# Turning q by VectorE in blocks of 32 partitions, the left tokens attended along, and buffers given by urgency

## The chip, the cores and the metric

The kernel runs on one core of one Trainium2 chip. The metric is the time of one execution on the device, in microseconds (us). Everything is in float32. A core has TensorE (PE, matrix products), VectorE (DVE), ScalarE (ACT), GpSimd (POOL), SyncE (SP, which issues most transfers) and 16 DMA engines.

## What is computed

Linear attention with a norm, and then a mixture of four experts of two layers each:

```
kv  = einsum('bhsd,bhse->bhde', k, v)            # batch 8, heads 8, seq 576, head_dim 64
out = einsum('bhsd,bhde->bhse', q, kv)
rms = sqrt(mean(out * out, axis=-1) + 1e-06)
att = out / rms * g_norm
x   = att with heads side by side                # 4608 tokens x 512
p   = domain_probs / (domain_probs.sum(-1) + 1e-09)
y   = sum over e of p[:, e] * (relu(x @ w1[e]) @ w2[e])   # w1: 512 x 1024, w2: 1024 x 512
```

Each batch has 576 tokens. The kernel works on blocks of 512, so the first 512 tokens of each batch make one block ("chunk" c = 0 to 7), and the 64 **left tokens** of all eight batches make a ninth. There are 36 stages: four experts times nine chunks. Attention runs only in the stages of expert 0: while stage s does the MoE work of chunk s, the attention of batch s + 1 is done beside it. The x of each chunk is stored to DRAM for the later experts.

## The kernel before

The MoE products use a scheme with fewer products and more additions (sums and differences of blocks, made by VectorE and GpSimd), over two levels in most stages. All its products go through one helper, which gives TensorE the two column halves in turn:

```
def halves_of(out_, lhsT, rhs, **kw):            # L356 in the profile
    for half in range(2):
        cols = slice(half * D, (half + 1) * D)   # D = 64
        nc.tensor.matmul(out_[cols], lhsT=lhsT[:, cols], rhs=rhs, **kw)
```

A float32 product leaves two records in the trace, a transpose one.

The kernel doesn't issue its operations as they are written. Each is handed to a **planner** with a key (the stage at which it is wanted), an assumed cost on each engine that may do it, and the buffers that it reads and writes. The planner walks through time with these costs, picks for each free engine an operation within reach of the oldest one, gives out buffers, and so fixes each engine's order before the kernel runs:

```
REACH = {"PE": 0.7, "DVE": 0.9, "ACT": 0.9, "POOL": 0.9, "SP": 1.0}
...
def ready(op, eng):
    ...                                          # all that it depends on is placed
    for k, n in need.items():                    # n new buffers of kind k
        spare = self.SPARE.get(k, 0) if k != "xf" or op.key < self.FORMS else 0
        if len(free[k]) < n + (spare if eng == "SP" and op.key > front + 0.1 else 0):
            return None
...
for op in pending:
    if op.key > reach: break
    ...
    if best is not None and op.due >= best.due: continue
    when = ready(op, eng)
    if when is None: continue
    if when > t: heapq.heappush(wake, when); continue
    best = op
    if eng in ("PE", "SP"): break
```

PSUM has eight banks: two each of `u1` and `u2` (first layer), `db` (second layer) and `ab` (attention; and the second layer in later stages). SBUF has 31 buffers `big` of 128x1024, and smaller kinds.

```
BANKS = {"u1": 2, "u2": 2, "db": 2, "ab": 2}
slots["small"] = [small_flat[:, i * NT:(i + 1) * NT] for i in range(8)]    # NT = 512
```

Attention of a batch, for pairs of heads hp = 0 to 3. q is loaded with tokens on partitions, turned by TensorE, and copied to SBUF by ScalarE:

```
for r in range(2):                               # b >= 1
    load(want, qt, lambda ...: qt.ap[:].rearrange("p (r h d) -> p r h d", h=2, d=D)[:, :, r, :],
         q[b, 2 * hp + r, 0:NT, :].rearrange("(p r) d -> p r d", r=NR), 128)
...
def turn(eng, bank=bank, qt=qt):                 # L693 for b >= 1; L697 for b = 0
    for r in range(NR):                          # NR = 4
        rs = slice(r * P, (r + 1) * P)
        if b:
            nc.tensor.transpose(bank.ap[:, rs], qt.ap[:, rs], ident[:])
            continue
        ...
plan.add(at(hp), act(NT), lambda ...: nc.scalar.activation(out=qT.ap[:], in_=bank.ap[:], func=ACT.Copy), ...)
def key_values(...):                             # L716: k'v of two pairs into one bank
    ...
def attend(eng, raw=raw, kv=kv, pairs=pairs):    # L743
    for o, hp in enumerate(pairs):
        for i in range(NR):
            for c in range(2):
                for r in range(2):
                    half = slice(r * D, (r + 1) * D)
                    at = i * P + c * D
                    nc.tensor.matmul(raw[r].ap[c * D:(c + 1) * D, (o * NR + i) * D:(o * NR + i + 1) * D],
                        lhsT=qTs[hp].ap[half, at:at + D], rhs=kv.ap[half, o * D:(o + 1) * D])
```

Then `scaled` takes the squares (ScalarE, from PSUM, two of 512), sums them per head (VectorE, 1024), takes the power -0.5 (GpSimd), and multiplies (VectorE, from PSUM, two of 512). Last, x is turned back, one group of four for each pair:

```
def turn_x(eng, bank=bank, x=x, o=o):            # L761
    for r in range(NR):
        nc.tensor.transpose(bank.ap[:, rs], x.ap[:, o * NT + r * P:o * NT + (r + 1) * P], ident[:])
```

The left tokens of the batch go through the same steps by themselves: their q is loaded and turned (L787, four transposes of 64x64), attends (L805, eight products, whose rows take 64 partitions), is scaled, and turned back (L821, four transposes).

Of the kernel before, what the change touches and what calls it, by code (L numbers as in the profile page):

```python
# [25 lines left out]
class Op:  # L26
    def __init__(self, key, cost, fn, reads, writes, kb, port):
        self.key, self.cost, self.fn, self.kb, self.port = key, cost, fn, kb, port
        self.outs = list(writes)
        self.bufs = list(dict.fromkeys(list(reads) + self.outs))  # L30
        self.deps = {}
        self.start = self.end = self.eng = None
        self.marks = self.seed = None


class Plan:
# [12 lines left out]
    REACH = {"PE": 0.7, "DVE": 0.9, "ACT": 0.9, "POOL": 0.9, "SP": 1.0}  # L49
# [4 lines left out]
    SLOW = 6.8  # L54

# [3 lines left out]
    def add(self, key, cost, fn, reads=(), writes=(), parts=(), kb=0, after=(), port=False, holds=()):  # L59


        op = Op(key, cost, fn, reads, list(writes) + list(parts), kb, port)
        for o in after:
            op.deps[o] = True
        for b in reads:
            for w in b.writers:
                op.deps[w] = True
            b.readers.append(op)
        for b in writes:
            for o in b.writers + b.readers:  # L70
                if o is not op:
                    op.deps[o] = True
            b.readers, b.writers = [], [op]
        for b in parts:
            b.writers.append(op)
        for b in holds:
            b.readers.append(op)
            op.bufs.append(b)
        for b in op.bufs:
            b.left += 1  # L80
        self.ops.append(op)
        return op

    def layout(self, slots, later, idle, idle_banks, idle_until):
# [25 lines left out]
        for op in reversed(self.ops):  # L110
            for d in op.deps:
                cross = self.SAME if op.cost.keys() == d.cost.keys() else self.CROSS
                d.due = min(d.due, op.due - cross - min(d.cost.values()))
        busy = {e: 0.0 for e in todo}
# [7 lines left out]
        def ready(op, eng):  # L122
            when = 0.0
            for d in op.deps:
                if d.start is None:
                    return None
            for d in op.deps:
                when = max(when, d.end + (self.SAME if d.eng == eng else self.CROSS))
            need = {}
            for b in op.outs:  # L130
                if b.kind is not None and b.slot is None:
                    need[b.kind] = need.get(b.kind, 0) + 1
            for k, n in need.items():
                spare = self.SPARE.get(k, 0) if k != "xf" or op.key < self.FORMS else 0
                if len(free[k]) < n + (spare if eng == "SP" and op.key > front + 0.1 else 0):
                    return None
                when = max(when, sorted(free[k])[n - 1][0])
            if eng == "SP":
                when = max(when, lanes[0])
            if op.port:  # L140
                when = max(when, port)
            return when

        while left:
# [4 lines left out]
            for eng in todo:  # L149
# [8 lines left out]
                best = None  # L158
                for op in pending:
                    if op.key > reach:  # L160
                        break
                    if op.start is not None:
                        continue
                    if best is not None and op.due >= best.due:
                        continue
                    when = ready(op, eng)
                    if when is None:
                        continue
                    if when > t:
                        heapq.heappush(wake, when)  # L170
                        continue
                    best = op
                    if eng in ("PE", "SP"):
                        break
                if best is not None:
# [14 lines left out]
                    for b in op.outs:  # L190
                        if b.kind is not None and b.slot is None:
                            free[b.kind].sort()
                            b.slot = free[b.kind].pop(0)[1]
                            b.ap = slots[b.kind][b.slot]
                    for b in op.bufs:
# [47 lines left out]
def kernel(  # L243
# [76 lines left out]
    for kind, n in BANKS.items():  # L320
# [8 lines left out]
    small_home = pool.tile([P, 4, 2 * NT], F32, tag="small", name="small")  # L329
    kv_flat = kv_home[:].rearrange("p n x -> p (n x)")  # L330
    small_flat = small_home[:].rearrange("p n x -> p (n x)")
    slots["kv"] = [kv_flat[:, i * KV:(i + 1) * KV] for i in range(4)]
    slots["kvbd"] = [kv_flat[:, 4 * KV + i * P:4 * KV + (i + 1) * P] for i in range(4)]
    slots["small"] = [small_flat[:, i * NT:(i + 1) * NT] for i in range(8)]
# [3 lines left out]
        (("small",), "w2y", [small_home[:, i, :] for i in range(2)]),  # L338
        (("small",), "big", [small_home[:, i, :] for i in range(2, 4)]),
# [21 lines left out]
    def act(n):  # L361
        return {"ACT": 0.155 + 0.00088 * n}
# [29 lines left out]
    def norm_probs(key):  # L392
        by_batch = moe_domain_probs.rearrange("(b s) e -> s b e", s=S)

        def load_all(eng):
            nc.sync.dma_start(
                out=p_all[:, 0:B * NR, :].rearrange("p (b r) e -> p b (r e)", r=NR),
                in_=by_batch[0:NT].rearrange("(p r) b e -> p b (r e)", r=NR),
            )
            for bb in range(2):  # L400
                nc.sync.dma_start(
                    out=p_all[bb * REM:(bb + 1) * REM, B * NR:NBLK, :],
                    in_=by_batch[NT:S, bb::2, :],
                )
# [10 lines left out]
        plan.add(key, {"SP": 1.8}, load_all, writes=[probs], kb=72)  # L415
# [204 lines left out]
    def attention(b, key, span, rem):  # L620
# [9 lines left out]
        splits = ((120, 4, 0), (96, 1, 480)) if b else ((96, 6, 0),)  # L630

        def load_pair(hp):
            hs = slice(2 * hp, 2 * hp + 2)
            n = f"{b}_{hp}"
            kind = "kv" if b else "big"
            kt, vt, qt = Buf(kind, f"k{n}"), Buf(kind, f"v{n}"), Buf("small", f"q{n}")
            want = at(hp) - 0.25 if b else key - 1 + 0.1 * hp
            if b == 0:
                load(
                    want, qt, lambda qt=qt: qt.ap[:].rearrange("p (h x) -> p h x", h=2),  # L640
                    q[b, hs, 0:NT, :].rearrange("h (p r) d -> p h (r d)", r=NR), 172,
                )
            else:
                for r in range(2):
                    load(
                        want, qt,
                        lambda qt=qt, r=r: qt.ap[:].rearrange(
                            "p (r h d) -> p r h d", h=2, d=D)[:, :, r, :],
                        q[b, 2 * hp + r, 0:NT, :].rearrange("(p r) d -> p r d", r=NR), 128,
                    )  # L650
            for t, src in ((kt, k), (vt, v)):
                at_ = 0
                for rows, n_, size in splits:
                    kb = rows * n_ // 2
# [5 lines left out]
                        kb if b else 241,  # L660
# [15 lines left out]
        groups = ((0,), (1,), (2,), (3,)) if b == 0 else ((0, 1), (2, 3))  # L676
        for g, pairs in enumerate(groups):
# [4 lines left out]
            for o, hp in enumerate(pairs):  # L682
# [4 lines left out]
                qT = qTs[hp] = Buf("small", f"qT{b}_{hp}")  # L687

                def turn(eng, bank=bank, qt=qt):
                    for r in range(NR):  # L690
                        rs = slice(r * P, (r + 1) * P)
                        if b:
                            nc.tensor.transpose(bank.ap[:, rs], qt.ap[:, rs], ident[:])  # L693
                            continue
# [8 lines left out]
                    at(hp), pe(4, P, 1) if b else {"PE": 0.82}, turn, reads=[qt], writes=[bank])  # L703
# [3 lines left out]
                        out=qT.ap[:], in_=bank.ap[:], func=ACT.Copy),  # L707
# [3 lines left out]
            def key_values(eng, bank=kbank, held=held):  # L711
# [12 lines left out]
                at(pairs[-1]), {"PE": (0.61 if b else 0.73) * size + 0.2}, key_values,  # L724
# [8 lines left out]
            kind = ("db", "u2", "u1", "db")[g] if b == 0 else "ab" if b > 1 else "db"  # L733
# [21 lines left out]
            for o, hp in enumerate(pairs):  # L755
                bank = Buf("ab", f"xT{b}_{hp}")

                def turn_x(eng, bank=bank, x=x, o=o):
# [13 lines left out]
                    reads=[bank] + ([gains] if b == 0 else []), parts=[xh],  # L772
# [4 lines left out]
        qr = Buf("small", f"qr{b}")  # L777
        load(
            at(1), qr, lambda: qr.ap[0:REM, :].rearrange("p (h d) -> p h d", d=D),
# [3 lines left out]
        qTr = Buf("small", f"qT{n}")  # L783
# [14 lines left out]
        rawr = [Buf("ab" if b else "db", f"raw{n}_{r}") for r in range(2)]  # L798
# [16 lines left out]
        xr = Buf("small", f"x{n}")  # L815
# [3 lines left out]
        def turn_xrem(eng):  # L819
            for cc in range(NPAIR):  # L820
# [11 lines left out]
                out=xs.ap[:], in_=xb.ap[:, 0:HN], func=ACT.Copy, scale=gcol[:]),  # L832
            reads=[xb], writes=[xs],
# [20 lines left out]
    def x_forms(c, key):  # L854
# [12 lines left out]
        for j, (o, a, b) in enumerate(((5, 12, 1), (6, 3, 5), (7, 3, 12), (4, 2, 6))):  # L867
            combine(
                key + (0.25, 0.26, 0.65, 0.8)[j], either(NT), blocks[o][1], blocks[a][1],
# [67 lines left out]
    last, inner_last, primed = [], [], []  # L937
# [158 lines left out]
    def result(s, e, c, base):  # L1096
# [9 lines left out]
        def rows(i):  # L1106
            if c < B:
                return [(slice(0, P), out[c * S:c * S + NT, :].rearrange(
                    "(p r) d -> p r d", r=NR)[:, i, :])]
# [63 lines left out]
    def down(s, e, c, mixed=False):  # L1173
# [5 lines left out]
        second = []  # L1179
        for t in range(2):  # L1180
            banks = {}
            for j, m in enumerate(order):
# [8 lines left out]
                def product(eng, m=m, t=t, ps=ps):  # L1191
# [10 lines left out]
                    after=second[-1:] if t and m in (1, 5) else (),  # L1202
                )
                op.marks = ps, HN
# [16 lines left out]
    def down_deep(s, e, c, groups=((1, 6), (7, 5), (4, 2), (3,)), base=None, h=None, merge=None, send=None):  # L1221
# [10 lines left out]
        for i, group in enumerate(groups):  # L1232
# [34 lines left out]
            for j, mm in enumerate(ORDER):  # L1267
# [3 lines left out]
                def product(eng, group=group, mm=mm, ps=ps, forms=forms):  # L1271
# [16 lines left out]
                    after=(inner_last[-2:-1] or primed) if mm == 1 else seeds if mm == 5 else (),  # L1288
                )
                op.marks, op.seed = (ps, n * P), mm == 2  # L1290
                if mm == 3:
                    inner_last.append(op)

# [96 lines left out]
    attention(0, -2.0, 1.3, 0.1)  # L1390
# [100 lines left out]
```

## Time and profile before

| | |
|---|---|
| time, median of 3 runs | 1689.58 us (1687.08 to 1689.68) |
| the profiled execution | 1687.81 us, span 1685.7 us |
| granted TensorE clock | 1.0 of full speed throughout |
| VectorE, ScalarE, GpSimd busy | 74%, 58%, 42% of the span |
| DMA | 234 MB, mean 139 GB/s |

The profile has a page of totals, a list of groups of instructions (line, engine, operation, output<-inputs, shape, count; then busy us and mean ns of one; then idle time ahead), a list of who waited for whom, a table of busy time by stretch, and a timeline. "PE" is TensorE's matmul, "PEld" its weight load. Names of tiles are without their numbers: `u` is both `u1` and `u2`. Matmuls overlap in TensorE's pipe, so the time that one group takes from the others is read from starts: the start of the next group less its own.

### The profile page before, as it was taken

Reading aid. Unit: us, or ns where it says so; the run is one execution under the profiler, and the core shown is the slowest. Engines: PE = TensorE matmul, PEld = TensorE weight load, DVE = VectorE, ACT = ScalarE, POOL = GpSimd, SP = SyncE. Lnnn points to the kernel's source line nnn. Section 1 sums busy time; section 2 is a strip of 40 time slices with the busy share of each in tenths; the row PEclk is TensorE's granted clock in tenths of the full one; section 3 lists DMA queues with packets and bytes.
Section 4 is the critical chain, followed back from the end, with each engine's and each line's share of the span. In section 5 each row is a group of like instructions: output and inputs, shape, how many; then the busy total and the mean of one; then the engine's idle time right before and its main releaser. Section 6 shows DMA issues by size and latency. Waiting matters only on the chain.

```text
span 1685.7 us, 66495 instructions
## 1 busy us (share of the span) xinstructions
PE 1677.6 (100%) x29038; PEld 1572.0 (93%) x29038; DVE 1239.6 (74%) x2045; ACT 975.4 (58%) x2405; POOL 714.9 (42%) x672
## 2 busy tenths in 40 slices
PE   9999999999999999999999999999999999999998
PEld 6687888888889999999999999999999999999996
DVE  4865665575787788777787787877787886877774
ACT  3454555455455666566666566666666666666662
POOL 3613333333444344334455445444446446444431
PEclk9999999999999999999999999999999999999999
DMA  9955553642566344444568444445478444444442
GB/s 236 265 180 151 166 158 101 200 148 94 199 154 166 112 115 115 115 115 114 129 179 198 115 115 115 115 115 114 111 188 200 122 114 115 115 115 115 115 102 51
DMA packets 172330, 234.27 MB, mean 139 GB/s; under 512 B 61576, under 2 KB 112648, under 8 KB 172040
## 3 DMA queue, kind: packets, MB, share of 16 engines
q1 hardware_dynamic: 148968, 193.32, 36.7%
q0 software_dynamic: 23072, 36.71, 15.1%
q8 instruction: 228, 3.74, 0.9%
q14 instruction: 62, 0.51, 0.1%
HBM read 155.79 MB, written 74.19 MB: 136 GB/s over the span
## 4 chain that ended last, share of the span: by engine, by line
PE 98%; DMA 1%; SPq 0%; issue 0%; ACT 0%; DVE 0%
PE u L356 47%; PE db L356 32%; PE ab L356 14%; PE ab L716 1%; PE ab L761 1%; PE ab L693 1%; DMA small<-in_q_dram 1%; PE ab L743 1%; DMA xf<-x 0%; PE ab L805 0%; PE ab L787 0%; PE db L743 0%; PE ab L821 0%; PE ab L1440 0%; SPq L385 0%
## 5 line engine op out<-in xcount | busy, mean ns | idle before, releaser
L379 DVE TENSOR_TENSOR big<-big,big 128x1024 f32<-128x1024 f32 (+1 forms) x517 | 502.0, 985 | 43.3 <-ACT big L959 16.7
L356 PE MATMUL u<-xf,big 128*64 128x128 f32 x7072 | 505.0, 273 | 0.6 <-DMA xf<-x 0.6
L356 PEld LDWEIGHTS u<-xf,big 128*64 128x64 f32 x7072 | 409.4, 137 | 5.2 <-issue 0.9
L356 PE MATMUL u<-xf,w1y 128*64 128x128 f32 x5304 | 382.8, 273 | 0.0
L356 PE MATMUL db<-big,big 128*64 128x128 f32 (+1 forms) x4328 | 362.0, 307 | 0.0
L1003 DVE TENSOR_TENSOR big<-u,snap 128x256 f32<-128x256 f32 x464 | 194.0, 420 | 214.4 <-PE u L356 149.2
L356 PEld LDWEIGHTS u<-xf,w1y 128*64 128x64 f32 x5304 | 307.6, 137 | 4.5 <-issue 1.3
L356 PEld LDWEIGHTS db<-big,big 128*64 128x64 f32 x4328 | 264.4, 137 | 39.3 <-issue 0.5
L995 ACT ACTIVATE snap<-u 128x256 f32<-128x256 f32 x490 | 187.0, 382 | 194.5 <-PE u L356 140.6
L379 POOL TENSOR_TENSOR big<-big,big 128x256 f32<-128x256 f32 (+1 forms) x156 | 192.0, 1234 | 168.9 <-DVE big L379 75.0
L995 ACT ACTIVATE big<-u 128x256 f32<-128x256 f32 x464 | 176.7, 383 | 89.7 <-PE u L356 69.3
L379 POOL TENSOR_TENSOR big<-big 128x512 f32<-128x512 f32 (+1 forms) x76 | 95.3, 1255 | 161.4 <-DVE big L379 104.4
L1304 ACT ACTIVATE snap<-db 128x256 f32<-128x256 f32 (+1 forms) x230 | 82.1, 357 | 114.7 <-PE db L356 102.4
L959 ACT ACTIVATE big<-big 128x1024 f32<-128x1024 f32 x133 | 139.8, 1051 | 4.7 <-DVE big L379 4.3
L1161 POOL DMA_DIRECT2D out_dram<-big x98 | 88.4, 1025 | 56.0 <-ACT big L1138 43.6
L1312 DVE TENSOR_TENSOR big<-ab,snap 128x256 f32<-128x256 f32 x164 | 69.0, 421 | 58.2 <-PE ab L356 28.4
L1342 POOL TENSOR_TENSOR big<-big 128x512 f32<-128x512 f32 x34 | 44.0, 1296 | 154.1 <-DVE big L379 140.8
L995 ACT ACTIVATE u<-u 128x256 f32<-128x256 f32 x245 | 91.0, 372 | 28.6 <-PE u L356 14.1
L379 DVE TENSOR_TENSOR big<-big 128x512 f32<-128x512 f32 (+1 forms) x121 | 103.1, 855 | 0.5 <-ACT big L1138 0.2
L356 PE MATMUL ab<-big,big 128*64 128x128 f32 (+1 forms) x1352 | 94.7, 277 | 0.1
L356 PE MATMUL db<-small,big 128*64 128x128 f32 x1240 | 90.6, 273 | 0.0
L356 PE MATMUL ab<-kv,big 128*64 128x128 f32 x1200 | 83.2, 273 | 0.0
(178 smaller groups left out, 2412.4 us busy)
## 6 DMA issues: line engine op xcount, KB each, us to landing
xf<-x SPq DMA_DIRECT2D x108, 512.0 KB, 3.7
out_dram<-big POOLq DMA_DIRECT2D x82, 256.0 KB, 5.6
xf<-x_h SPq DMA_DIRECT2D x81, 256.0 KB, 3.5
xf<-x SPq DMA_DIRECT2D x81, 256.0 KB, 3.9
x<-xf SPq DMA_DIRECT2D x36, 512.0 KB, 4.9
big<-in_moe_w_dram SPq DMA_DIRECT2D x31, 512.0 KB, 5.2
x_h<-big SPq DMA_DIRECT2D x18, 512.0 KB, 3.4
big<-in_moe_w_dram POOLq DMA_DIRECT2D x17, 512.0 KB, 7.5
```

What stands on the lines that cost most here:

```text
L356: nc.tensor.matmul(out_[cols], lhsT=lhsT[:, cols], rhs=rhs, **kw)
L379: lambda eng: adder(eng).tensor_tensor(out=out_(), in0=a(), in1=b(), op=op),
L693: nc.tensor.transpose(bank.ap[:, rs], qt.ap[:, rs], ident[:])
L716: nc.tensor.matmul(bank.ap[r * D:(r + 1) * D, o * D:(o + 1) * D], lhsT=ks[r], rhs=vs[r], start=(j == 0), stop=(j == len(sets) - 1), skip_g ...
L743: nc.tensor.matmul(raw[r].ap[c * D:(c + 1) * D, (o * NR + i) * D:(o * NR + i + 1) * D], lhsT=qTs[hp].ap[half, at:at + D], rhs=kv.ap[half, ...
L959: lambda eng: nc.scalar.activation(out=b.ap[:], in_=b.ap[:], func=ACT.Relu),
L995: lambda eng: nc.scalar.activation(out=where(), in_=ps.ap[:, 0:HN], func=ACT.Copy),
L1003: lambda eng: nc.vector.tensor_tensor(out=block(whole, a, t), in0=src.ap[:, 0:HN], in1=add_.ap[:], op=ALU.add),
L1161: nc.gpsimd.dma_start(out=dst, in_=cell(i)[parts, :], accum_op=ALU.add)
L1304: lambda eng: nc.scalar.activation(out=where(), in_=group_of(ps.ap), func=ACT.Copy),
L1312: lambda eng: nc.vector.tensor_tensor(out=cell(tq, dq), in0=group_of(src.ap), in1=group_of(add_.ap), op=ALU.add,),
L1342: lambda eng: adder(eng).tensor_tensor(out=whole(to), in0=whole(a), in1=whole(b), op=ALU.add),
```

## The change

It has two parts.

**Attention of the batches 1 to 7 is written anew** (batch 0 keeps the old way, in a function of its own, with `big` buffers for its q). A batch is done in two half batches s of four heads each. q comes in by eight loads per half batch: 32 of a head's 64 dimensions of 32 tokens form a block, and each of the four sets of 32 partitions holds one half of the dimensions of one head. All 576 tokens come in together. VectorE then turns all the 32x32 blocks in place, with one instruction of 1152 columns, after which dimensions stand on the partitions:

```
+    for r in range(2):
+        for dh in range(2):
+            a = 2 * r + dh
+            for o in range(2):
+                load(when - 0.3, qt,
+                    lambda qt=qt, a=a, o=o: qt.ap[a * R:(a + 1) * R, o * S:(o + 1) * S]
+                    .rearrange("p (n d) -> p n d", d=R),                       # R = 32, S = 576
+                    q[b, 4 * s + 2 * o + r, :, dh * R:(dh + 1) * R].rearrange("(n p) d -> p n d", p=R), 140)
+    plan.add(when - 0.1, dve(QW),                                              # QW = 1152
+        lambda eng, qt=qt: nc.vector.transpose(out=qt.ap[:], in_=qt.ap[:]), reads=[qt], writes=[qt])
```

The left tokens attend in the same operation as the others. It writes both `ab` banks and, for the left tokens, both `db` banks:

```
+    raw = [Buf("ab", f"raw{n}_{r}") for r in range(2)]
+    rest = [Buf("db", f"rest{n}_{r}") for r in range(2)]
+    def attend(...):
+        ...                                      # 32 products as before, into raw
+        for o in range(2):
+            col = o * S + NT
+            for r in range(2):
+                half = slice(r * D, (r + 1) * D)
+                nc.tensor.matmul(rest[r].ap[s * D:(s + 1) * D, o * D:(o + 1) * D],
+                    lhsT=qt.ap[half, col:col + D], rhs=kv.ap[half, o * D:(o + 1) * D])
+    plan.add(at(2 * s + 1.0), {"PE": 1.45}, attend, reads=[qt, kv], writes=raw + rest, early=True, gang=True)
```

ScalarE or VectorE, as the planner chooses, copies the results out of PSUM: `raw` into the buffer that held q, `rest` into a buffer with both half batches' left tokens on 128 partitions. Squares go to an `ab` bank (twice 512), VectorE sums them, GpSimd takes the power, VectorE multiplies in place (one of 1024), and TensorE turns x back in one operation of eight transposes per half batch. The left tokens of the whole batch are scaled together (256 wide) and turned back with two transposes of 128x128. The tokens of a block now lie on the partitions in order, so the stores of `out` and the load of the probabilities change:

```
-    return [(slice(0, P), out[c * S:c * S + NT, :].rearrange("(p r) d -> p r d", r=NR)[:, i, :])]
+    if c:
+        return [(slice(0, P), out[c * S + i * P:c * S + (i + 1) * P, :])]
+    return [(slice(0, P), out[0:NT, :].rearrange("(p r) d -> p r d", r=NR)[:, i, :])]
...
-    nc.sync.dma_start(out=p_all[:, 0:B * NR, :]..., in_=by_batch[0:NT].rearrange("(p r) b e -> p b (r e)", r=NR))
+    nc.sync.dma_start(out=p_all[:, 0:NR, :], in_=moe_domain_probs[0:NT, :].rearrange("(p r) e -> p r e", r=NR))
+    for r in range(NR):
+        nc.sync.dma_start(out=p_all[:, NR + r:B * NR:NR, :], in_=by_batch[r * P:(r + 1) * P, 1:, :])
```

The eight `small` buffers become two `q` buffers of 1152 columns and three `small` ones.

**The planner gives out buffers by urgency.** TensorE's reach grows to 1.1 stages. A `big` buffer isn't given to an operation while more urgent ones (by their due time) wait for one; `xf` buffers are given in the order of due times; and while an attending operation (`gang`) could start but for its banks, no operation that would open a new MoE bank of such a kind may take it:

```
-    REACH = {"PE": 0.7, ...}
+    REACH = {"PE": 1.1, ...}
+    SHARED, AHEAD, INORDER = ("big",), 0.3, ("xf",)
...
+    if k in waiting and len(free[k]) < n + claimed(k, op):
+        return None
+    if k in first and any(o.due < op.due for o in first[k] if o is not op):
+        return None
...
+    if op.opens and any(b.kind in kept for b in op.outs):
+        continue
     when = ready(op, eng)
     if when is None:
+        if op.gang and all(d.start is not None and d.end < t for d in op.deps):
+            kept.update((b.kind, True) for b in op.outs if b.kind in BANKED)
         continue
```

In the second layer of the stages of expert 0, a fixed order is set between the first operations of successive groups of products (`second`, `firsts`), so that groups from different stages don't hold one bank each.

## The prediction

> **What bounds the kernel now.** I read the page's head first, then what TensorE waited for, then a table by stage, then the groups of TensorE by shape, then the timeline of one stretch. The head:
>
> ```profile
> span 1685.7 us, 66495 instructions
> ## 1 busy us (share of the span) xinstructions
> PE 1677.6 (100%) x29038; PEld 1572.0 (93%) x29038; DVE 1239.6 (74%) x2045; ACT 975.4 (58%) x2405; POOL 714.9 (42%) x672
> ```
>
> TensorE is busy for 1677.6 of 1685.7 us. That alone proves little, since the ends of matmuls are modelled, so I ask for its waits:
>
> ```profile
> PE ab L1440 <- POOL ident masks.py:199: 1.4, 1, 1.4
> PE ab L697 <- DMA small<-in_q_dram: 1.0, 2, 0.6
> PE u L356 <- DMA xf<-x: 0.6, 1, 0.6
> PE ab L821 <- ACT big L769: 0.3, 1, 0.3
> ```
>
> All of TensorE's waits sum to 3.3 us (columns: us in total, times, longest). No other engine's time can be bought back here: VectorE could be halved and the end would hardly move. Two stretches, 160 to 400 us with attention and 600 to 840 us without (columns PE, PEld, DVE, ACT, POOL busy, clock, DMA share, GB/s):
>
> ```profile
> 160.00:400.00 240.00, 240.00 (x3912) 201.16 (x3908) 145.66 (x268) 128.54 (x297) 86.57 (x71) 1.00 0.44 137
> 600.00:840.00 240.00, 240.00 (x4402) 240.00 (x4400) 187.04 (x276) 148.71 (x377) 101.78 (x100) 1.00 0.47 116
> ```
>
> TensorE is full in both, with VectorE at 61% and 78%. So the time is the sum of what TensorE is given to do, and the change is worth what it takes out of that sum. The attention's own groups on TensorE (L693 turns q, L716 makes k'v, L743 attends, L761 turns x back, L787, L805 and L821 do the same for the 64 left tokens):
>
> ```profile
> L761 PE MATMUL ab<-ident,big 128*128 128x128 f32 x128 | 20.2, 284 | 0.0
> L693 PE MATMUL ab<-ident,small 128*128 128x128 f32 x112 | 18.1, 284 | 0.1
> L743 PE MATMUL ab<-kv,small 64*64 64x64 f32 x768 | 13.9, 221 | 0.0
> L805 PE MATMUL ab<-kv,small 64*64 64x64 f32 x112 | 4.8, 224 | 0.0
> L787 PE MATMUL ab<-ident,small 64*128 64x64 f32 x32 | 3.7, 235 | 0.0
> L821 PE MATMUL ab<-ident,small 64*128 64x64 f32 x32 | 3.7, 235 | 0.3 <-ACT big L769 0.3
> ```
>
> The mean of 284 ns is the length of one in the pipe, not its cost. The cost is the step from its start to the next start. One piece of the timeline shows it:
>
> ```profile
> 173.22 0.61 PE L356 MATMUL u<-xf,w1y 128*64 128x128 f32 x8
> 173.65 0.61 PE L356 MATMUL u<-xf,big 128*64 128x128 f32 x8
> 174.19 0.66 PE L693 MATMUL ab<-ident,small 128*128 128x128 f32 x4
> 174.78 0.66 PE L356 MATMUL u<-xf,w1y 128*64 128x128 f32 x8
> 175.26 0.94 PE L356 MATMUL db<-big,big 128*64 128x128 f32 x14
> ```
>
> A group of eight MoE records steps by 0.43 us undisturbed (173.22 to 173.65). Ahead of the four transposes the same group takes 0.54, the transposes take 0.59, and the group after them takes 0.48. So four transposes cost 0.59, and going in and out of them another 0.10 + 0.05. Over 80 to 420 us I summed the steps of MoE records above their floor (54.35 ns for 128 columns, 106.7 for 256): 11.0 us, of which 1.7 would be there without attention (0.0059 of the MoE time, as from 560 to 1000 us). The other 9.4 us over 68 returns to MoE work make 0.138 us per **switch**, and there are about 9.3 of them per batch.
>
> **What the Trainium skill says.** "TensorEngine Tiling (Array Packing)", Key Properties: "Mode switching requires drain". The MoE products are 128*64, the transposes 128*128 and the attending products 64*64, so each such step changes mode; the trace agrees, with the 0.138 us above. "VectorE: DVE Perf Modes", The three transpose paths: VectorE turns 32x32 blocks only, into SBUF, while TensorE turns a whole 128x128 but into PSUM. That is why the change puts halves of 64 dimensions on 32 partitions each. "Vector Engine (DVE) Microarchitecture Reference", 3.8, says that such a transpose sustains one element per cycle per lane; no row of this trace has one. "DMA: Bandwidth & Descriptors", Specifications, puts the least transfer for full rate at 512 B. The trace agrees in kind: its 256 B packets take 19 ns on average, its 1024 B packets 63 ns, its 16 B packets 9.5 ns, so a quarter of the bytes costs a third of the time.
>
> **The change part by part, on TensorE, for one of the batches 1 to 7.** Steps from start to start, summed over the trace.
>
> Removed: the four groups that turn q, 28 groups in 16.1 us, 0.575 each, **2.30 us**. The turn of the left tokens' q, **0.39**. The left tokens' own attending group (L805) of 16 records, 0.61.
> Added: the left tokens' 16 records now ride on the two attending groups. There a record costs 17.4 ns (1024 in 17.8 us) when four quadrants of the array work; the added ones use only one column half, so I take twice that: 2 x 8 x 0.035 = 0.56, a saving of only **0.05**.
> Turning x back: eight transposes in one group, where it was four. A transpose steps by 0.109 and the last of a group by 0.203, so 7 x 0.109 + 0.203 = 0.97, twice, 1.93 against the 2.28 of now (18.2 us over 8 batches): **0.35**. The left tokens go back with two 128-wide transposes, 0.31 against 0.41: **0.10**.
> Unchanged: k'v (L716), 2.42.
> Switches: 15 operations of attention made 9.3 switches, as some stand next to each other; 7 operations are left (two k'v, two attends, two turns, one for the left tokens). I choose 6 switches, so 3.3 fewer at 0.138: **0.46**.
> Sum: 2.30 + 0.39 + 0.05 + 0.35 + 0.10 + 0.46 = 3.65 us a batch, times 7 = **25.6 us**. 1689.6 less 25.6 is 1664.0.
>
> Beside TensorE, so free as long as it stays beside: VectorE gets two transposes of 1152 columns per batch. The trace's 1024-wide reduction takes 1.21 us, so by the skill's rate I estimate 1.35 us, 2.7 a batch. It also shares the new copies out of PSUM with ScalarE (ScalarE's 512-wide copy takes 0.60). ScalarE loses four such copies and gets four. The multiplication by the norm moves from two 512-wide with a PSUM source (0.68 each) to one of 1024. In some 51 us of a stage this lifts VectorE from 61% to some 67%. DMA: q of a batch is 9216 packets of 128 B where it was 4608 of 256 B. The latter cost 4608 x 19 ns / 16 = 5.5 us of all 16 engines; at 12 to 19 ns for 128 B (an estimate between the 16 B and 256 B packets) the new cost is 7 to 11.
>
> The reordering ("buffers go to the most urgent operation", longer reach for TensorE, locks on order) adds no work. In a stream that waits for 3.3 us it can win back at most a few us: the 0.5 us gap at the load of the left tokens near 529 us, and something of the start. I count 0. The 1150 us after 540 us have no attention and run within 0.6% of the floor, so nothing comes from there.
>
> **The rivals.** (1) *A new wait for banks.* Attending now wants four banks at once: both `ab` and both `db`. Until now it took two, and `db` is where the second MoE layer works in these stages. So that layer must have drained, and it stays out until the left tokens' rows are copied. TensorE then has only the first layer to run, whose products wait for ScalarE's copies (0.38 us each). Against it: the planner's order has held TensorE without waits so far, and the change adds rules that keep banks for such an operation. If 0.5 us is lost 14 times, the time is 1671; if 1.5 us, 1685. (2) *A longer chain of each half batch*: load, transpose, attend, copy, square, reduce, power on GpSimd (2.9 us for 16 columns), multiply, turn, all in one buffer of which there are two. A stage of 51 us has room for it, which speaks against. (3) *The start.* From 20 to 80 us the DMA engines are 94 to 100% busy, and two batches of q with double the packets fall into or near it, as do the probabilities, now with 3584 packets of 16 B where 896 of 64 B did. It could push a needed load by 3 to 10 us: 1667 to 1674. For it: the load. Against it: TensorE lacks almost nothing there now. (4) *VectorE's transpose is several times dearer*, 5 us instead of 1.35: 10 us a stage would not fill VectorE's 20 idle us, but would make single waits; some 1675. (5) *More than the sum*: all switches gone but four, the gap and the start improved: 1656.
>
> **Range and chances.** The point is 1664. Below it there is little room: the removed work is counted, and 2% (1655.8) would need 34 us, a third more than the sum. Above it lie rivals 1 and 3. Range 1656 to 1678. Faster by over 2%: 0.07. Within 2%: 0.90. Slower by over 2% (1723) would need TensorE to lose 60 us that it doesn't lose now: 0.03.
>
> **What would show it.** In the profile after: no transposes of q by TensorE but batch 0's; about 8.2 us of attention and switches per batch where it was 11.9; groups of eight transposes that step by about 0.97 us; VectorE's transposes near 1.35 us; the stretch without attention unchanged; the list of TensorE's waits still under 10 us. The prediction is wrong if that list shows waits for ScalarE or VectorE at the attending products or at the second layer's first product (rival 1), for q's loads (rival 3), or if the MoE steps rise above 54.4 ns where the first layer runs alone.

## The result and the profile after

The changed kernel takes 1665.3 us (median of 4 runs, 1664.63 to 1666.04) against 1689.25 us; the ratio is 0.9861, with a 95% interval from 0.9844 to 0.9878. The prediction was 1664, from 1656 to 1678. The profiled execution has a span of 1664.0 us, 21.7 less than before. First the head of the page of after:

```profile
span 1664.0 us, 66253 instructions
## 1 busy us (share of the span) xinstructions
PE 1651.2 (99%) x28884; PEld 1557.9 (94%) x28884; DVE 1250.9 (75%) x2051; ACT 972.7 (58%) x2391; POOL 705.1 (42%) x701
```

TensorE is still the bound, but it now idles for 12.8 us of the span where it idled for 8.1. Its list of waits is longer (columns: us in total, times, longest):

```profile
PE ab L1069 <- DVE ss L933: 1.6, 1, 1.6
PE ab L761 <- issue: 1.5, 1, 1.5
PE ab L1712 <- POOL ident masks.py:199: 1.4, 1, 1.4
PE ab L1090 <- DVE snap L950: 1.0, 1, 1.0
PE ab L1069 <- DVE small L950: 0.8, 1, 0.8
```

L1069 turns x back and L1090 the left tokens' x. L761 belongs to batch 0. Before, the longest wait of the attention was 0.6 us. The table by stretch of after, with the stretches of the prediction's table and the start (columns PE, PEld, DVE, ACT, POOL busy, clock, DMA share, GB/s):

```profile
40.00:80.00 40.00, 36.87 (x463) 20.91 (x464) 31.19 (x57) 15.35 (x38) 21.59 (x13) 1.00 0.76 193
160.00:400.00 240.00, 240.00 (x4046) 206.58 (x4044) 180.37 (x295) 132.76 (x304) 97.03 (x109) 1.00 0.55 163
600.00:840.00 240.00, 240.00 (x4402) 240.00 (x4400) 178.59 (x279) 151.27 (x380) 94.71 (x95) 1.00 0.49 124
```

From 160 to 400 us TensorE is full as before, and it gets 4046 records into the stretch instead of 3912. From 600 to 840 us it has 4402 records, the same as before. In the start, 40 to 80 us, it lacks 3.1 us, where it lacked 0.5. VectorE stands at 75% in the second row, where it had 61%.

The new groups: on TensorE those of the batches 1 to 7 (L1028 the attending products, L1037 the left tokens' ones that ride along), on VectorE the transpose of q:

```profile
L1028 PE MATMUL ab<-kv,small 64*64 64x64 f32 x896 | 16.3, 221 | 0.0
L1069 PE MATMUL ab<-ident,small 128*128 128x128 f32 x112 | 15.5, 280 | 2.4 <-DVE ss L933 1.6 <-DVE small L950 0.8
L1037 PE MATMUL db<-kv,small 64*64 64x64 f32 x112 | 5.6, 218 | 0.0
L1090 PE MATMUL ab<-ident,snap 128*128 128x128 f32 x14 | 3.1, 301 | 1.0 <-DVE snap L950 1.0
L975 DVE STREAM_TRANSPOSE small<-small 128x1152 f32<-128x1152 f32 x14 | 19.2, 1370 | 0.0
```

The counterpart of the prediction's piece of timeline is an attending operation of after:

```profile
149.82 0.67 PE L410 MATMUL u<-xf,big 128*64 128x128 f32 x8
150.42 1.16 PE L1028 MATMUL ab<-kv,small 64*64 64x64 f32 x64
151.42 0.40 PE L1037 MATMUL db<-kv,small 64*64 64x64 f32 x8
151.75 0.66 PE L410 MATMUL u<-small,w1y 128*64 128x128 f32 x8
152.24 0.61 PE L410 MATMUL u<-small,big 128*64 128x128 f32 x8
```

The 64 records step by 1.00 us and the left tokens' 8 by 0.33. There is one way in and one way out for both (the first MoE group behind them steps by 0.49). Before, the left tokens had a group, and a change of mode, of their own.

Summing TensorE's steps from start to start gives the account:

| us, from TensorE's first record to its last | before | after |
|---|---|---|
| 26 800 MoE records at their floor | 1558.9 | 1558.9 |
| MoE records above the floor (switches, waits) | 21.3 | 21.0 |
| attention of batches 1 to 7 | 74.2 | 52.1 |
| batch 0, and fill at the start | 24.9 | 26.0 |
| number of returns to MoE work (switches), not us | 83 | 52 |

The whole gain stands in the third row. 31 switches fewer, at the prediction's 0.138, should have taken 4.3 us from the second row; it fell by 0.3, so some 4 us of new waits stand there. The largest are single steps of MoE records: 1.8 us above the floor ahead of L1069 at 62.4 us and 1.0 at 125.6, 1.3 ahead of L1090 at 72.0, and two of 0.6 at the end (1633.1 and 1634.2 us).

### The profile page after: what moved, and what is told of

The parts are those of the page before. It is cut to its first block, busy times and chain, and to the rows that moved or that the text cites. A ratio compares the mean times of both kernels' runs of the same rounds, so it can differ in the third digit from the quotient of the medians.

```text
span 1664.0 us, 66253 instructions
## 1 busy us (share of the span) xinstructions
PE 1651.2 (99%) x28884; PEld 1557.9 (94%) x28884; DVE 1250.9 (75%) x2051; ACT 972.7 (58%) x2391; POOL 705.1 (42%) x701
## 4 chain that ended last, share of the span: by engine, by line
PE 96%; DMA 1%; POOL 1%; DVE 1%; SPq 1%; issue 0%; ACT 0%; DVEq 0%; POOLq 0%; ACTq 0%
PE u L410 46%; PE db L410 32%; PE ab L410 15%; PE ab L1001 1%; PE ab L1069 1%; DMA big<-in_v_dram 1%; PE ab L1028 1%; POOL rt L944 1%; DMA big<-in_moe_w_dram 0%; SPq L439 0%; POOL big L433 0%; DVE big L433 0%; SPq L455 0%; POOL ss L940 0%; PE ab L1090 0%
## 5 line engine op out<-in xcount | busy, mean ns | idle before, releaser
L433 DVE TENSOR_TENSOR big<-big,big 128x1024 f32<-128x1024 f32 (+1 forms) x527 | 518.8, 1001 | 34.1 <-ACT big L1226 15.9
L410 PE MATMUL u<-xf,big 128*64 128x128 f32 x6784 | 486.9, 273 | 0.2
L410 PEld LDWEIGHTS u<-xf,big 128*64 128x64 f32 x6784 | 393.9, 137 | 5.4 <-issue 1.0
L1270 DVE TENSOR_TENSOR big<-u,snap 128x256 f32<-128x256 f32 x476 | 199.5, 421 | 209.1 <-PE u L410 136.4
L433 POOL TENSOR_TENSOR big<-big,big 128x256 f32<-128x256 f32 (+1 forms) x196 | 219.1, 1134 | 222.9 <-DVE big L433 118.4
L433 POOL TENSOR_TENSOR big<-big 128x512 f32<-128x512 f32 (+1 forms) x76 | 94.5, 1250 | 114.8 <-DVE big L433 82.0
L410 PE MATMUL db<-small,big 128*64 128x128 f32 (+1 forms) x1552 | 116.9, 274 | 0.0
L1429 POOL DMA_DIRECT2D out_dram<-big x108 | 94.4, 1004 | 50.1 <-ACT big L1406 47.8
L433 DVE TENSOR_TENSOR big<-big 128x512 f32<-128x512 f32 (+1 forms) x131 | 101.1, 783 | 2.4 <-PE u L410 2.3
L1614 POOL TENSOR_TENSOR big<-big 128x512 f32<-128x512 f32 x21 | 26.8, 1276 | 173.6 <-DVE big L433 140.9
L1406 ACT ACTIVATE big<-big,p_all 128x256 f32<-128x256 f32 x200 | 94.5, 501 | 5.4 <-POOL big L1614 4.0
L410 PEld LDWEIGHTS db<-small,big 128*64 128x64 f32 x1552 | 91.3, 137 | 0.7
```

The source lines that it names most:

```text
L433: lambda eng: adder(eng).tensor_tensor(out=out_(), in0=a(), in1=b(), op=op),
L1270: lambda eng: nc.vector.tensor_tensor(out=block(whole, a, t), in0=src.ap[:, 0:HN], in1=add_.ap[:], op=ALU.add),
L1406: lambda eng: nc.scalar.activation(out=cell(i, half), in_=ap(), func=ACT.Copy, scale=prob()),
L1429: nc.gpsimd.dma_start(out=dst, in_=cell(i)[parts, :], accum_op=ALU.add)
L1614: lambda eng: adder(eng).tensor_tensor(out=whole(to), in0=whole(a), in1=whole(b), op=ALU.add),
```

## The experiments

Theory: the time is the sum of TensorE's work, and what the change takes out of that sum is the gain. Rivals: the planner's rules are part of the gain; VectorE is nearly the bound; the start hangs on the transfers.

**1. The rules alone.** The old attention with the planner of after (and its fixed order in the second layer):

```
+ REACH["PE"] = 1.1; SHARED = ("big",); INORDER = ("xf",); gang / opens / second / firsts
  attention() as before
```

> The old attention with all of the new planner rules (reach 1.1, buffers by urgency, order of xf, bank locks, order of the second layer's groups). Theory (the gain is TensorE work taken out; the rules only reorder): no work is taken out, so within 4 us of before, 1685 to 1693 us. Rival (the rules win back hidden waits and are half of the gain): 1677 or less.

Measured: 1687.32 us, ratio to before 0.9992 (0.9984 to 1.0001). The rules by themselves bring nothing that can be told from zero. The lock on banks had nothing to act on here, as no operation of the old attention is marked `gang`.

**2. The attention alone.** The new attention with the old reach, and without urgency and order; the lock on banks and the order of groups stay, so no run shows what these two are worth:

```
- "PE": 1.1          SHARED, INORDER = ("big",), ("xf",)
+ "PE": 0.7          SHARED, INORDER = (), ()
```

> The new attention with the old reach of 0.7, and without the urgency of big buffers and the order of xf; the bank lock and the order of the second layer's groups stay, as without them the plan deadlocks. Theory: the whole gain is here, 1662 to 1670 us. Rival (the rules carry half of the gain): 1675 or more.

Measured: 1674.06 us, ratio 0.9916 (0.9899 to 0.9933). That is 8.8 us above after: neither theory's number, though nearer to the rival's. Zero alone and 8.8 us together means that the three rules taken out here win back what the new attention would lose. This run's timeline of all engines shows most of it in one place:

```profile
59.61 0.40 PE L1037 MATMUL db<-kv,small 64*64 64x64 f32 x8
...
60.12 3.75 POOL L944 TENSOR_TENSOR rt<-ss,mhalf 128x16 f32<-128x16 f32 x1
...
61.23 1.10 ACT L927 ACTIVATE ab<-small 128x512 f32<-128x512 f32 x2
...
63.91 1.23 DVE L950 TENSOR_TENSOR small<-small,rt 128x1024 f32<-128x1024 f32 x1 [1.31 <-POOL rt L944]
...
65.49 1.29 DVE L933 TENSOR_REDUCE ss<-ab 128x8 f32<-128x512 f32 x2
...
66.23 1.11 PE L1069 MATMUL ab<-ident,small 128*128 128x128 f32 x4 [6.23 <-DVE ss L933]
```

TensorE attends for one half batch, and then stands for 6.2 us ahead of the turn back of the other. GpSimd's power ends at 63.9, VectorE then multiplies (L950), and only then sums the squares (L933) that ScalarE had put into both `ab` banks at 61.2; the turn back needs those banks. In this plan TensorE was given no MoE work in between. From 40 to 80 us it lacks 8.7 us, 5.6 more than after; most of the rest, by the estimate at runs 6 and 7, is a lower clock.

**3. The removed work put back.** TensorE turns q's buffer again ahead of the products, into the banks that the products then overwrite:

```
  def attend(...):
+     for o in range(2):
+         for t in range(NR):
+             nc.tensor.transpose(raw[o].ap[:, t * P:(t + 1) * P],
+                 qt.ap[:, o * NT + t * P:o * NT + (t + 1) * P], ident[:])
```

> The changed kernel, in whose attending operation TensorE turns eight 128x128 blocks per half batch ahead of the products (their result is overwritten, the output stays right); the plan's order is unchanged. Theory (TensorE's time is a sum): 14 x (7 x 0.109 + 0.203) = 13.6 us more than after, 1679 us, or up to 2 us more for a further change of mode inside. Rival (the removed work had been hidden behind waits): under 7 us more.

Measured: 1679.01 us, 13.7 more than after. Work given to TensorE is paid in full.

**4. VectorE's transpose three times.**

```
- nc.vector.transpose(out=qt.ap[:], in_=qt.ap[:])
+ the same, three times in a row
```

> The changed kernel with VectorE's transpose of q done three times in a row (two cancel, the output stays right), the plan's order unchanged: 14 x 2 x 1.37 = 38 us more for VectorE. Theory (VectorE works beside TensorE with room left): 0 to 6 us more than after, by single waits where TensorE's fixed order meets late data. Rival (VectorE's chain is close to the bound): 15 to 38 us more.

Measured: 1687.69 us, ratio to before 1.0 (0.9991 to 1.0008): 22.4 us more than after, and all of the change's gain is gone. The theory's number was far off. Of this run, the top line of TensorE's waits, and then one such wait in the timeline of all engines:

```profile
PE u L410 <- DVE big L1270: 15.0, 9, 2.6
```

```profile
186.75 2.79 DVE L975 STREAM_TRANSPOSE small<-small 128x1152 f32<-128x1152 f32 x2
187.47 0.60 PE L410 MATMUL u<-small,big 128*64 128x128 f32 x8
...
189.78 0.41 DVE L1270 TENSOR_TENSOR big<-u,snap 128x256 f32<-128x256 f32 x1
190.24 0.66 PE L410 MATMUL u<-big,w1y 128*64 128x128 f32 x8 [2.17 <-DVE big L1270]
```

L1270 is the addition that empties a bank of the first layer. VectorE's order is fixed, so it stands behind the transposes, and TensorE waits for the bank.

**5. The same, with the planner told.** The three transposes are planned at 3.9 us instead of 1.35.

> Three transposes in a row as in the run before, but the planner is told 3.9 us for them instead of 1.35 and so lays the order anew. Theory A (VectorE has room; TensorE lost 22 us only because the fixed order met late data, the first layer's banks being freed behind the transposes): within 6 us of after, 1665 to 1671 us. Theory B (VectorE's room in these stages is truly used up): 1677 us or more.

Measured: 1669.55 us, ratio 0.9888 (0.9872 to 0.9905). With the same 38 us more for VectorE, 18 of the 22 us come back. So VectorE does have the room. 18 of the 22 us were the price of a fixed order laid for a shorter operation.

**6 and 7. Which rule wins back the 8.8 us.** The changed kernel without the urgency of `big` buffers (6: `SHARED = ()`), and with the short reach (7: `"PE": 0.7`).

> The changed kernel without the urgency of big buffers; reach 1.1 and the order of xf stay. If the urgency of big buffers is what won back the 8.8 us (the long wait near 60 us at the start, and the end), 1672 to 1676 us; if it is the reach or the order of xf, 1664 to 1668 us.

> The changed kernel with TensorE's reach back at 0.7; urgency and the order of xf stay. If the longer reach is what won the 8.8 us, as it gives TensorE work of the first layer beside an attending operation, 1671 to 1676 us; if not, 1664 to 1668 us.

Measured: 1670.67 and 1671.8 us, 5.4 and 6.5 more than after. Run 6 lies between its two forecasts, run 7 within the one for a reach that counts. Both rules count, and their parts (11.9) don't add up to 8.8; the order of `xf` wasn't taken out alone. They act in different places. The stretch where run 6 lost, and then the one of run 7:

```profile
480.00:540.00 60.00, 56.60 (x990) 55.35 (x988) 44.92 (x90) 30.94 (x78) 18.40 (x18) 0.97 0.55 147
```

```profile
40.00:80.00 40.00, 35.70 (x460) 20.07 (x458) 32.55 (x60) 16.13 (x40) 22.27 (x13) 0.96 0.77 193
```

Without urgency TensorE lacks 3.4 us from 480 to 540 us, where the changed kernel lacks nothing and attention is over. With the short reach it lacks 4.3 us in the start, 1.2 more than after.

Idle time isn't all of the loss. The granted clock, the seventh number, is 0.97 and 0.96 here, and 1.00 in these stretches of after. In run 6 it fell to 0.5 from 497.7 to 501.1 us, behind two waits of about 1 us:

```profile
496.76 0.66 PE L410 MATMUL u<-xf,w1y 128*64 128x128 f32 x8 [0.85 <-DVE big L1270]
...
499.41 1.07 PE L410 MATMUL u<-xf,w1y 128*64 128x128 f32 x8
500.26 1.01 PE L410 MATMUL u<-xf,big 128*64 128x128 f32 x8
```

Eight MoE records step by 0.85 us there (499.41 to 500.26) instead of 0.44. So 3.4 us at half the clock cost some 1.7 us (an estimate from these steps), and with the 3.4 us of idle time that is nearly all of run 6's 5.4. Run 7's trace has two such stretches of 3.4 us (from 17.6 and 65.4 us), run 4's two (from 131.8 and 241.1 us), and run 2's one of 6.8 us, half of it spent idle, and one of 3.4 (from 62.8 and 76.4 us). Runs 5 and 12 have one each, before and after none but at the very start and end. A wait in runs 2, 4, 6 and 7 therefore seems to cost more than its own length. When the clock falls isn't shown (after waits for 1.6 us ahead of L1069 without it). The rest of run 7's loss is spread.

**8. The probabilities loaded as before.** One transfer of 64 B pieces for the first 512 tokens of all batches (they then belong to other tokens than the rows), with the same planned order:

```
- out=p_all[:, 0:NR, :] ... and four of p_all[:, NR + r:B * NR:NR, :]
+ out=p_all[:, 0:B * NR, :]...  in_=by_batch[0:NT].rearrange("(p r) b e -> p b (r e)", r=NR)
```

> The changed kernel with the probabilities loaded as before, in one transfer of 64 B pieces where five of 16 and 64 B stand (they then belong to other tokens than the rows, so the output is not the reference's); the plan's order is the same. Theory (the start's new waits of TensorE hang on SyncE's queue, which spends 6 us on these transfers ahead of the second layer's weights): 2 to 4 us less than after, 1661 to 1663 us. Rival (the waits at 62 to 74 us hang on GpSimd's powers alone): no difference, within 1 us.

Measured: 1665.08 us, 0.2 from after, with runs from 1664.33 to 1668.81 (the highest had a mean clock of 0.998, the others 0.999 to 1.0). In the single profile TensorE's step ahead of L1069 near 62 us is 0.97 us instead of 1.93, but the time doesn't show it. The forecast of 2 to 4 us less failed; the rival's, within 1 us, held.

**9 and 10. GpSimd in the start.** The chain that ended last, in the start of after (start, us, what):

```profile
48.70 6.08 DMA big<-in_moe_w_dram
...
54.93 2.38 POOL big L433
...
57.39 1.07 POOL ss L940
...
58.54 3.76 POOL rt L944
...
62.33 1.24 DVE small L950
...
63.70 2.35 POOL big L433
...
66.69 3.76 POOL rt L944
```

It runs through GpSimd's sums of the second layer's weights (L433) and its powers (L944), with weights that have just landed. Run 9 gives those sums to VectorE alone (`dve(1024)` for `either(1024)` where the first expert's w2 sums are formed); run 10 does so too, and plans the powers at 0.4 + 0.2 us a column for 0.3 + 0.19.

> The changed kernel with the four 1024-wide sums of the first expert's second-layer weights given to VectorE alone (GpSimd takes 2.4 us for one and stands ahead of the powers at 54 to 66 us). If GpSimd's queue is what TensorE waits for at 62 to 74 us: 2 to 4 us less than after, 1661 to 1663 us. If VectorE, which then has 2.4 us more to do there, takes its place: within 1 us of after or above it.

> As the run before, and the planner is told 0.4 + 0.2 us a column for the powers, nearer to the 3.5 us that a half batch's take, instead of 0.3 + 0.19. If the leftover waits come from work that the plan thinks shorter than it is: 1659 to 1663 us. Else as the run before.

Measured: 1663.58 us (0.9857, 0.984 to 0.9873) and 1666.97 us (0.9878, 0.9863 to 0.9892). Run 9 is 1.7 us under after, but its interval covers after's ratio, so it isn't shown to be better. Run 10 missed its forecast (1659 to 1663): it is 3.4 us above run 9, so the higher cost for the powers didn't help. In the start a half batch's power and the step ahead of it take 1.07 + 3.76 us in the lines above, and 3.6 was planned. TensorE still lacks 2.9 us from 40 to 80 us there; what changed is the first 40 us. The cause of the start's 3 us stays open between the landing of the weights, GpSimd's powers and the planned order; q's own loads there weren't tested by a run.

**11 and 12. A visit to another mode, by itself.** In the 27 stages without attention, behind one product in seven of the first layer:

```
+ if mm == 4 and s >= NCH:                       # run 11
+     nc.tensor.transpose(ps.ap[:, HN:HN + P], ident[:], ident[:])
+     halves_of(ps.ap[:, HN:HN + P], ident[:], rhs=ident[:], ...)     # run 12, in its place
```

> The changed kernel with one 128x128 transpose of the identity put behind one product in seven of the first layer in the 27 stages without attention, into an unused quarter of its bank: 189 visits to another mode. From the steps of the trace of before: 189 x (0.203 + 0.138) = 64 us more, 1730 us. If the drain were no cost and only the transpose's own 0.109 counted: 21 us more, 1686 us.

> As the run before, but what is put in is a product of the identity with itself in the MoE's own 128x64 mode, four records of 128 columns: no change of mode. 189 x 4 x 0.0544 = 41 us more, 1706 us, with no extra step beside it.

Measured: 1743.22 us (ratio 1.0328, 1.0313 to 1.0343) and 1708.53 us (1.0123, 1.0107 to 1.0138). Against after, a visit costs 77.9 / 189 = 0.412 us, and the product in the MoE's own mode 43.2 / 189 = 0.229 (forecast 0.218). Run 11 is 13 us above its forecast of 1730, or 0.07 a visit. In the timeline of run 11:

```profile
700.01 0.61 PE L410 MATMUL u<-xf,big 128*64 128x128 f32 x8
700.54 0.33 PE L1249 MATMUL u<-ident 128*128 128x128 f32 x1
700.80 0.66 PE L410 MATMUL ab<-w2y,big 128*64 128x128 f32 x8
701.29 0.61 PE L410 MATMUL ab<-kv,big 128*64 128x128 f32 x8
701.73 1.04 PE L410 MATMUL u<-xf,w1y 128*64 128x128 f32 x16
```

The group ahead steps by 0.53 instead of 0.43, the one behind by 0.49, and the transpose alone by 0.26, where one amid others steps by 0.109. So the way in and out costs 0.15 us, near the prediction's 0.138, and the transpose's own step is 0.15 longer than that of one amid others. Groups of after show the two parts of this: the first transpose of a group steps mostly by 0.165 and the last by 0.203, so 0.056 and 0.094 more. The forecast had counted the last and not the first, which is 10.6 of its missing 13 us.

A transpose is also another operation than a product, so run 11 alone doesn't show that the mode is what costs. The trace of after does:

```profile
142.45 1.04 PE L410 MATMUL u<-xf,w1y 128*64 128x128 f32 x16
143.43 1.16 PE L1028 MATMUL ab<-kv,small 64*64 64x64 f32 x64
...
145.66 0.61 PE L410 MATMUL u<-xf,big 128*64 128x128 f32 x8
146.10 1.34 PE L1001 MATMUL ab<-kv 120*64 120x64 f32 x40
```

Neither L1028 nor L1001 (k'v) is a transpose. Ahead of L1028 (64*64) sixteen MoE records take 0.98 us instead of 0.87; ahead of L1001 (120*64, near the MoE's 128*64) eight take 0.44, as undisturbed. Over before and after, the last MoE record of 128 columns steps by 0.20 us ahead of all 20 attending groups that follow on one, and by 0.10 ahead of all 16 such groups of k'v. So k'v comes and goes without a switch.

## Why the prediction was right, point by point

**TensorE as the bound, and the sum as the measure: right.** Run 3 shows it by putting work back (13.7 us for a forecast of 13.6), run 12 by adding some (43.2 for 41). Where TensorE must wait, as in runs 2, 4, 6 and 7, the sum isn't all.

**The parts.** Forecast and measured, per batch:

| us | forecast | measured |
|---|---|---|
| q's turns and the left tokens' turn | 2.69 | 2.69 |
| the left tokens' attending group | 0.05 | 0.16 |
| x turned back | 0.35 | 0.20 |
| left tokens turned back | 0.10 | 0.05 |
| switches (measured: 31 fewer, at the forecast's 0.138) | 0.46 | 0.61 |
| k'v, taken as unchanged | 0.00 | 0.06 |
| sum | 3.65 | 3.77 |

Times 7 the measured sum is 26.4 us. The span fell by 21.7 us and the medians by 24. The **term that was mis-sized** is the new waits: I set them at nothing, and TensorE idles 4.7 us more (12.8 less 8.1), which is the difference of 26.4 and 21.7. That the point came within 1.3 us of the median is in part luck. Slightly more was removed than I counted, against the waits; and the four runs of before lie high: those beside the experiments have medians of 1688.07 to 1688.31, which makes the gain 23 us rather than 24.

Turning x back saved less than forecast for the reason that run 11 shows: I left out the dearer first transpose, so a group of eight steps by 1.02 us and not 0.97. The trace of before already had two such groups of 1.02 (at 259.3 and 372.8 us).

**"I count 0" for the reordering.** As a gain of its own, right (run 1). As a judgement of its worth, incomplete: with the new attention reach, urgency and the order of `xf` are worth 8.8 us (run 2). The change's two parts belong together.

**The rivals.** Rival 1, waits for banks at the attending operation, didn't come there: no wait of L1028 or L1037 stands in the list of after. The sign that I had named beside it, waits of the second layer for ScalarE or VectorE, does show in the trace of after: four of 0.2 to 0.4 us, 1.4 in all. None is for the copies that empty the left tokens' banks (L909, L910), and two are at 1633.8 and 1634.8 us, where no attention runs. Run 5 has one for such a copy, of 1.4 us. The lock was in all runs with the new attention, so its own worth wasn't measured.

But a wait for banks came at another place that I hadn't named: the squares sit in the `ab` banks, and the turn back (L1069) waits for their sum (L933; 1.6 us in the list, 6.2 in run 2). It is one with rival 2, the longer chain: that sum stands in VectorE's order behind the multiplication that waits for GpSimd's power. Against my argument, "a stage of 51 us has room for it" doesn't hold in the start, where the plan put too little other work beside it.

Rival 3, the transfers at the start: q's 128 B packets took 14.0 ns on average, so 8.1 us of all 16 DMA engines a batch, within my 7 to 11; the probabilities had no effect that shows in the time (run 8).

Rival 4: the transpose took 1.37 us where I had 1.35. That is 1.19 ns a column, as the reduction's 1.18 (1.21 us for 1024). It agrees with the element per cycle and lane that the Trainium skill states ("Vector Engine (DVE) Microarchitecture Reference", 3.8), as far as the reduction runs at that rate too. But my sentence that a dearer transpose would only make single waits, "some 1675", was too mild. 2.7 us more a half batch made it 1687.7 with the order unchanged (run 4), and 1669.6 with an order laid for it (run 5). VectorE's load in the attention stages was also more than I forecast: 75% from 160 to 400 us against some 67%.

**Mode switches.** What the Trainium skill says of the drain ("TensorEngine Tiling (Array Packing)", Key Properties) agrees with run 11, in stages that have no attention at all, so it isn't an effect of attention's waits. But not each return to MoE work is such a switch. My 0.138 is a mean of dear returns (0.10 ahead and 0.05 behind) and of free ones, those from k'v. Without the groups of k'v, the times that TensorE leaves MoE work fell from 74 to 39. At 0.15 each that is an estimate of 5.3 us instead of the 4.3 above, and of 5 us of new waits in the MoE records instead of 4. So the removed work is nearer to 27 us than to 26, and that the two figures of 4.7 us agree so closely is chance.

## What to carry to other kernels

Where one engine is full, read each group's cost from start to start, add the cost of entering and leaving its mode, and a change's worth follows as a sum. An engine beside the bound may have room on average and still stop it, when its order is fixed and a bank's release stands behind an operation that takes longer than planned: run 5 shows what it is worth to tell the planner of it (18 of 22 us), and run 10 that a higher cost for one operation doesn't always help. A wait can also cost more than its length: in runs 2, 4, 6 and 7 the clock was halved for 3.4 us or more near the waits. A rule of scheduling that is worth nothing alone can be what a change of the work needs in order to pay.

## What the runs showed of the hardware that I had not expected

A lone 128x128 float32 transpose between products of another mode costs 0.41 us of TensorE (run 11), nearly four times the 0.109 us of one amid others. Products of 120*64 between those of 128*64 cost no such step, while products of 64*64 do (0.10 us ahead of them). And VectorE's transpose of 1152 float32 columns on 128 partitions runs in place in 1.37 us, a column in the same 1.19 ns as in a reduction of 1024 (1.21 us).
